# Padding the SBUF pools on both sides so that every FFN tile starts on a multiple of 1,024 bytes

## The chip, the cores and the metric

One core of a Trainium2 chip (trn2) runs the kernel. The time is device microseconds of one execution; the kernel before takes 1147.21 us (median of 3 runs, 1147.18 to 1148.46).

## What is computed

Attention with rotary embedding over 4 batches, 8 heads, 576 positions and 64 dimensions per head, then two feed-forward layers (FFN) over the 2,304 resulting tokens of width 512, with a hidden width of 2,048. All values are float32.

```python
def _attn_ref(q, k, v):            # (4, 8, 576, 64)
    ...
    scores = scale * np.matmul(q_rot, k_rot.transpose(0, 1, 3, 2))
    attn = np.exp(scores - np.max(scores, axis=-1, keepdims=True))
    attn = attn / (np.sum(attn, axis=-1, keepdims=True) + 1e-09)
    return np.matmul(attn, v)

def _moe_ref(x, w_in, w_out):      # layer 1
    h = x @ w_in
    return (h - np.tanh(h)) @ w_out

def _moe2_ref(x, w_in, w_out):     # layer 2
    h = x @ w_in
    return (h * (1.0 / (1.0 + np.exp(-h)))) @ w_out
```

## The kernel before

**Attention** goes over 16 pairs of heads, nine score tiles each. A pair's rotated queries and keys (`qs`, `kh`, `kl`, `qr`) lie in the pool `qk_even` for the pairs 0, 2, 4, ... and in `qk_odd` for the others. Once per pair a transposition `tpr` (L402) turns the reciprocals of its row sums. While attention runs, a converter (`Conv`) turns the FFN weights into a high and a low fp32r part each (L121 to L153, ACT, DVE and POOL).

**The FFN** follows from about 328 us on. Tokens are cut into five blocks `kb`: four of 512 tokens and one of 256. There are four passes `p`: passes 0 and 1 are the two halves of layer 1's hidden width, passes 2 and 3 those of layer 2. The table `SEQ` lists pass, block and `f`, one of the eight slices of 128 hidden columns of a half; each entry is one call of `tick`. A tick of a 512-token block issues two groups on TensorE:

- `gemm_h` (L685): twelve matmuls, `w_in` chunks as the weights, the block's input as the streamed operand: for each of four chunks `win` high by `xh`, `win` high by `xl`, `win` low by `xh`.
- `gemm_out` (L761) for the tick four before: three matmuls for each of `na` accumulators. In passes 0 and 1 `wout` is loaded as weights and `gh`/`gl` are streamed; in passes 2 and 3 `gh`/`gl` are loaded as weights and `wout` is streamed.

So TensorE runs twelve matmuls of L685 and twelve of L761 in turn. Before each matmul its weights (128 x 128) are loaded by an instruction of their own. Between the two groups ACT and DVE work the activation out (L696 to L730: `t`, `u`, `s`, `mk`, `gh`, `gl`). The order is written out by hand in `tick`; no table or scheduler moves it.

**Where the tiles lie.** SBUF is filled from two sides. The left side takes the pools `const`, `stage`, `wearly`, then attention's own tiles and `qk_odd`, whose place `wlate`, `ffn_out` and `ffn_x` take over after attention. The right side takes `qk_even` and `rope`, whose place the pool `ffn` takes over. A tile's address is the sum of the sizes ahead of it. In the built program `const` holds 512 + 32 + 32 bytes per partition behind a start at 16,512, so that the first tile after it, `raw`, begins at byte 17,088, which is 704 past a multiple of 1,024. All later FFN tiles of the left side (`wa`, `wm`, `win`, `wout`, `xo`, and the `xh`, `xl` of `ffn_x`) are multiples of 1,024 bytes long and begin at 704 past such a multiple as well. The right side ends at the end of SBUF; its FFN tiles (`xin`, the other `xh` and `xl`, `t`, `u`, `s`, `mk`, `gh`, `gl`) all begin at 992 past a multiple of 1,024.

An input block's `xh` and `xl` alternate between the sides (`split`, L665 to L671):

```python
        fp = pools["sb" if x % 2 == 0 else "x"]
        hi = fp.tile([128, T], F32R, tag=f"xh{c}", name=f"xh{c}", bufs=1)
        lo = fp.tile([128, T], F32R, tag=f"xl{c}", name=f"xl{c}", bufs=1)
```

`pools["sb"]` is the right side, `pools["x"]` the left; `x` counts the input blocks as they are loaded. Of the 128 ticks of 512-token blocks 72 stream their input from the right side and 56 from the left. Of those 56, 24 lie in layer 1 and 32 in layer 2. The weights `win` and `wout` are always on the left, `gh` and `gl` always on the right.

Of the kernel before, what the change touches and what calls it, by code (L numbers as in the profile page):

```python
# [8 lines left out]
F32 = mybir.dt.float32  # L9
# [20 lines left out]
def kernel(  # L30
# [39 lines left out]
    const = ctx.enter_context(tc.tile_pool(name="const", bufs=1))  # L70
# [3 lines left out]
    make_identity(nc, ident)  # L74
    sqa = const.tile([128, 1], F32, name="sqa")
    ht2 = const.tile([128, 1], F32, name="ht2")
    dram = ctx.enter_context(tc.tile_pool(name="dram", bufs=1, space=bass.MemoryType.DRAM))

    xd = [[dram.tile([128, KD, TW[kb]], F32, name=f"xd{l}{kb}") for kb in range(NBLK)] for l in range(2)]
# [820 lines left out]
```

## Time and profile before

| | |
|---|---|
| time, median of 3 runs | 1147.21 us (1147.18 to 1148.46) |
| span of the profiled execution | 1145.9 us |
| TensorE (PE) busy | 1119.5 us, 98% |
| weight loads (PEld) busy | 902.6 us, 79% |
| VectorE (DVE) busy | 785.3 us, 69% |
| ScalarE (ACT) busy | 659.2 us, 58% |
| GpSimd (POOL) busy | 268.4 us, 23% |
| mean granted TensorE clock | 0.999 |

The profile gives the profiled execution's time as its span, from the first instruction to the last; the median of the timed runs lies 1.3 us above that. A matmul's duration in the profile (about 394 ns for 512 columns) is longer than the distance from its start to the next one's start: neighbours overlap. What a matmul costs in a row of many is that distance, which the timeline shows.

### The profile page before, as it was taken

The numbers are of one execution on the slowest core, as the hardware profiler recorded it, in microseconds if no ns is written. First come the engines' busy times: TensorE is split into PE (matmuls) and PEld (weight loads), VectorE is DVE, ScalarE is ACT, GpSimd is POOL, SyncE is SP. The second block draws the span as 40 slices with busy tenths as digits, with TensorE's granted clock in tenths as the row PEclk, the third lists the DMA queues.
The fourth block names the chain that finished last, engine by engine and source line by source line (L and its number), as shares of the span: only waits on it lengthen the run. The fifth ranks groups of instructions, "written<-read, shape, count | busy, mean of one in ns | idle before, by whom it ended". The sixth has DMA issues, their size and how long they took to land.

```text
span 1145.9 us, 16928 instructions
## 1 busy us (share of the span) xinstructions
PE 1119.5 (98%) x6032; PEld 902.6 (79%) x6032; DVE 785.3 (69%) x1385; ACT 659.2 (58%) x1431; POOL 268.4 (23%) x359
## 2 busy tenths in 40 slices
PE   5999999999999999999999999999999999999998
PEld 4777777777778889888888898888888888888887
DVE  7778788787858978888899979876544533323323
ACT  4888888788866757766666657534343323222221
POOL 6566676666300101111001001111000000000000
PEclk9999999999999999999999999999999999999999
DMA  4133323232311223221333332432232203122012
GB/s 130 47 99 84 113 68 110 89 94 86 100 64 42 92 74 111 96 89 56 111 129 110 111 120 84 147 111 92 75 110 74 74 1 111 37 74 93 31 44 74
DMA packets 69588, 98.94 MB, mean 86 GB/s; under 512 B 13952, under 2 KB 50432, under 8 KB 67712
## 3 DMA queue, kind: packets, MB, share of 16 engines
q1 hardware_dynamic: 69344, 97.61, 26.3%
q8 instruction: 47, 0.77, 0.3%
q14 instruction: 37, 0.30, 0.1%
q10 hardware_dynamic: 160, 0.26, 0.1%
HBM read 74.25 MB, written 23.59 MB: 85 GB/s over the span
## 4 chain that ended last, share of the span: by engine, by line
PE 91%; DVE 4%; ACT 3%; issue 1%; DMA 0%; SPq 0%; POOL 0%; DVEq 0%; ACTq 0%
PE acc L761 35%; PE hp L685 35%; PE x L498 7%; PE tpp L466 4%; PE sc L364 3%; PE sc L365 2%; PE tpq L332 2%; PE sc L371 1%; ACT p L391 1%; DVE st L377 1%; ACT kh L346 1%; PE sc L446 1%; PE tpb L418 0%; DMA xm<-in_q_dram 0%; DVE wa L136 0%
## 5 line engine op out<-in xcount | busy, mean ns | idle before, releaser
L685 PE MATMUL hp<-xh,win 128*128 128x512 f32 (+1 forms) x1280 | 391.7, 371 | 0.0
L696 ACT ACTIVATE t<-hp 128x512 f32<-128x512 f32 (+1 forms) x160 | 89.0, 557 | 409.7 <-PE hp L685 400.0
L730 DVE TENSOR_TENSOR gl<-t,gh 128x512 fp32r<-128x512 f32 (+1 forms) x160 | 105.9, 662 | 259.5 <-ACT gh L728 259.2
L685 PEld LDWEIGHTS hp<-xh,win 128*128 128x128 f32 x1280 | 233.7, 188 | 46.8 <-issue 1.3
L685 PE MATMUL hp<-xl,win 128*128 128x512 f32 (+1 forms) x640 | 237.0, 370 | 0.0
L761 PE MATMUL acc<-gh,wout 128*128 128x512 f32 (+1 forms) x640 | 196.7, 372 | 1.2 <-ACT u L700 1.2
L761 PE MATMUL acc<-wout,gh 128*128 128x512 f32 x576 | 181.0, 395 | 0.0
L377 DVE TENSOR_REDUCE st<-sc 128x1 f32<-128x576 f32 x144 | 108.7, 755 | 60.0 <-PE sc L446 34.9
L685 PEld LDWEIGHTS hp<-xl,win 128*128 128x128 f32 x640 | 120.2, 188 | 23.2
L761 PEld LDWEIGHTS acc<-gh,wout 128*128 128x128 f32 x640 | 116.7, 188 | 24.9 <-ACT u L700 1.6
L761 PEld LDWEIGHTS acc<-wout,gh 128*128 128x128 f32 x576 | 107.1, 188 | 24.4
L761 PE MATMUL acc<-gl,wout 128*128 128x512 f32 (+1 forms) x320 | 118.9, 372 | 0.0
L153 POOL TENSOR_TENSOR win<-wa,win 128x512 fp32r<-128x512 f32 x32 | 45.4, 1419 | 292.5 <-ACT win L149 292.5
L761 PE MATMUL acc<-wout,gl 128*128 128x512 f32 x288 | 113.8, 395 | 0.0
L391 ACT ACTIVATE p<-sc,st 128x576 f32<-128x576 f32 x144 | 107.0, 743 | 9.4 <-DVE pr L434 7.2
L153 POOL TENSOR_TENSOR wout<-wa,wout 128x512 fp32r<-128x512 f32 x32 | 43.8, 1367 | 284.2 <-ACT wout L149 272.5
L432 ACT ACTIVATE pt<-tpp 128x512 f32<-128x512 f32 x144 | 86.1, 598 | 28.2 <-PE tpp L466 27.4
L728 ACT ACTIVATE gh<-t 128x512 fp32r<-128x512 f32 (+1 forms) x160 | 93.7, 586 | 1.5 <-PE acc L761 1.5
L364 PE MATMUL sc<-kh,qs 128*128 128x288 f32 x256 | 85.4, 348 | 7.1 <-ACT p L391 5.1
L466 PE MATMUL tpp<-ident,p 128*128 128x128 f32 x576 | 87.1, 274 | 0.0
L498 PE MATMUL x<-pt,vm 128*64 128x256 f32 (+1 forms) x512 | 75.8, 418 | 2.1 <-DVE xs L507 1.9
L364 PEld LDWEIGHTS sc<-kh,qs 128*128 128x128 f32 x256 | 49.2, 192 | 34.2 <-ACT p L391 17.8
(112 smaller groups left out, 1798.5 us busy)
## 6 DMA issues: line engine op xcount, KB each, us to landing
raw<-in_moe_w_in_dram SPq DMA_DIRECT2D x32, 512.0 KB, 3.6
raw<-in_moe_w_out_dram SPq DMA_DIRECT2D x32, 512.0 KB, 3.6
xin<-xd SPq DMA_DIRECT2D x14, 1024.0 KB, 4.8
pd<-xo SPq DMA_DIRECT2D x34, 256.0 KB, 2.7
xo<-pd SPq DMA_DIRECT2D x34, 256.0 KB, 4.9
xm<-in_k_dram SPq DMA_DIRECT2D x16, 256.0 KB, 2.9
xm<-in_q_dram SPq DMA_DIRECT2D x16, 256.0 KB, 3.0
vm<-in_v_dram SPq DMA_DIRECT2D x16, 256.0 KB, 2.9
```

What stands on the lines that cost most here:

```text
L153: POOL.tensor_tensor(out=w[:, 1], in0=self.val.pop(j), in1=w[:, 0].bitcast(F32), op=ALU.subtract)
L364: PE.matmul(sc[:, e, 0:HALF], lhsT=l, rhs=kh[:, c], start=True, stop=False)
L377: DVE.tensor_reduce(out=st, in_=s_t[g][:, :, 0:HALF], op=ALU.max, axis=AX.XY, negate=True)
L391: ACT.activation(out=p.rearrange("p (e s) -> p e s", e=2), in_=sc[:, :, 0:HALF], func=ACTF.Exp, bias=st, accum_out=sum_t[i][:, n:n + 1])
L432: ACT.activation(out=dst, in_=src, func=ACTF.Copy)
L466: PE.transpose(tp[:, cc * 128:(cc + 1) * 128], p[:, p0 + cc * 128:p0 + (cc + 1) * 128], ident)
L498: PE.matmul(x[o, 0:w], lhsT=l, rhs=r, start=(cc == 0), stop=(cc == NJ))
L685: PE.matmul(hp, lhsT=w[:, a, ws], rhs=bb, start=(n == 0), stop=(n == 3 * KD - 1))
L696: ACT.activation(out=t, in_=hp, func=ACTF.Tanh, scale=0.5 if l else 1.0)
L728: ACT.activation(out=gh, in_=t, func=ACTF.Copy)
L730: DVE.tensor_tensor(out=gl, in0=t, in1=gh.bitcast(F32), op=ALU.subtract)
L761: PE.matmul(acc, lhsT=a, rhs=bb, start=(fi == 0 and n == 0), stop=(fi == NH - 1 and n == 2))
```

## The change

Two tiles that nobody reads or writes are added: 80 float32 (320 bytes) per partition at the end of `const`, and a pool of its own on the right side with 248 float32 (992 bytes), opened before all others there.

```diff
     sqa = const.tile([128, 1], F32, name="sqa")
     ht2 = const.tile([128, 1], F32, name="ht2")
+    const.tile([128, 80], F32, name="pad_left")
+    right_pad = ctx.enter_context(tc.tile_pool(name="right_pad", bufs=1, side="right"))
+    right_pad.tile([128, 248], F32, name="pad_right")
     dram = ctx.enter_context(tc.tile_pool(name="dram", bufs=1, space=bass.MemoryType.DRAM))
```

Everything on the left behind `const` moves up by 320 bytes and everything on the right moves down by 992. All FFN tiles of both sides then begin on a multiple of 1,024. Tiles of one side keep their distances to each other; the distance between a tile on the right and one on the left falls by 1,312 bytes, which is just what was free between the sides. Attention's tiles move by the same amounts; those of `qk_even` come from 992, 480 and 224 past a multiple of 1,024 to 0, 512 and 256. On every engine the instructions, their order and their waits are the same as before; only addresses differ. Line numbers behind the added lines rise by 3.

## Rows read from the trace of the kernel before

**Rows 1.** Page: TensorE's busy time, and its granted clock in 40 slices
```profile
PE 1119.5 (98%) x6032; PEld 902.6 (79%) x6032; DVE 785.3 (69%) x1385; ACT 659.2 (58%) x1431; POOL 268.4 (23%) x359
...
PEclk9999999999999999999999999999999999999999
```

**Rows 2.** Groups by line and shape, TensorE: names, shapes, count | busy, mean ns | idle before
```profile
L685 PE MATMUL hp<-xh,win 128*128 128x512 f32 x1024 | 341.0, 394 | 0.0
L685 PE MATMUL hp<-xl,win 128*128 128x512 f32 x512 | 201.0, 393 | 0.0
L761 PE MATMUL acc<-wout,gh 128*128 128x512 f32 x576 | 181.0, 395 | 0.0
L761 PE MATMUL acc<-gh,wout 128*128 128x512 f32 x512 | 171.5, 396 | 1.2 <-ACT u L700 1.2
L761 PE MATMUL acc<-wout,gl 128*128 128x512 f32 x288 | 113.8, 395 | 0.0
L761 PE MATMUL acc<-gl,wout 128*128 128x512 f32 x256 | 101.1, 395 | 0.0
```

**Rows 3.** Waits of TensorE from 300 us to the end: total, times, longest
```profile
PE acc L761 <- ACT u L700: 1.2, 1, 1.2
```

**Rows 4.** Timeline of TensorE, layer 1, input on the right: start, us, instruction
```profile
717.85 0.63 PE L685 MATMUL hp<-xh,win 128*128 128x512 f32 x2
...
719.25 0.63 PE L685 MATMUL hp<-xh,win 128*128 128x512 f32 x2
...
720.65 0.63 PE L761 MATMUL acc<-gh,wout 128*128 128x512 f32 x2
...
722.05 0.63 PE L761 MATMUL acc<-gh,wout 128*128 128x512 f32 x2
```

**Rows 5.** Timeline of TensorE, layer 2, input on the left
```profile
940.79 0.61 PE L685 MATMUL hp<-xh,win 128*128 128x512 f32 x2
...
942.15 0.61 PE L685 MATMUL hp<-xh,win 128*128 128x512 f32 x2
```

**Rows 6.** Chain that ended last, in order of time: start, us, instructions
```profile
567.61 2.80 PE acc L761 x12
...
612.08 2.80 PE acc L761 x12
...
798.30 2.80 PE acc L761 x12
...
815.10 2.80 PE acc L761 x12
...
887.96 2.79 PE acc L761 x12
...
970.86 2.79 PE acc L761 x12
```

**Rows 7.** Timeline of TensorE, 256-token block: input on the right, then on the left
```profile
422.33 0.40 PE L685 MATMUL hp<-xh,win 128*128 128x256 f32 x2
...
423.04 0.40 PE L685 MATMUL hp<-xh,win 128*128 128x256 f32 x2
...
834.83 0.40 PE L685 MATMUL hp<-xh,win 128*128 128x256 f32 x2
...
835.54 0.40 PE L685 MATMUL hp<-xh,win 128*128 128x256 f32 x2
```

**Rows 8.** Windows (us, busy PE, PEld, DVE, ACT, POOL, clock, DMA); DVE's waits 560:700
```profile
570.00:590.00 20.00, 20.00 (x88) 16.21 (x87) 19.86 (x30) 12.83 (x24) 3.96 (x3) 1.00 0.41 132
...
DVE gl L730 <- ACT gh L728: 13.6, 11, 1.9
```

**Rows 9.** Timeline of TensorE: the transposition that each pair of heads has once
```profile
37.54 0.27 PE L402 MATMUL tpr<-ident,rr 128*9 128x128 f32 x1
...
56.98 0.27 PE L402 MATMUL tpr<-ident,rr 128*9 128x128 f32 x1
...
76.42 0.27 PE L402 MATMUL tpr<-ident,rr 128*9 128x128 f32 x1
```

## The prediction

> **What bounds the kernel now.** [...] Then its groups by shape: the 512-column matmuls of the FFN have no idle time ahead of them but for one wait of 1.2 us [rows 2], and from 300 us to the end that is TensorE's only wait of this size [rows 3]. From 328 us on the time is the number of matmuls times the distance between their starts. Nothing else has to be known about that stretch, and only something that alters this distance can alter the time.
>
> The change moves no instruction. So I asked the timeline whether the distance depends on where the operands lie, since the kernel itself holds a comparison: the same line, L685, with the same weights on the left, streams its input from the right side in some ticks and from the left in others.
>
> - Input on the right (it begins at 992 past a multiple of 1,024, the weights at 704): from 717.85 to 719.25 are six matmuls, 1.40 us or 233 ns each [rows 4].
> - Input on the left (704 and 704): from 940.79 to 942.15 are six matmuls, 1.36 us or 227 ns each [rows 5].
> - L761 in the same stretch as the first, streamed operand on the right, weights on the left: 720.65 to 722.05, again 1.40 us for six [rows 4].
>
> The chain of waits shows the same over whole ticks (twelve of L685 and twelve of L761). Three ticks with input on the right take 815.10 - 798.30 = 16.80 us, 5.60 each. Fifteen ticks of layer 2 with input on the left take 970.86 - 887.96 = 82.90 us, 5.527 each. Eight ticks of layer 1 with input on the left take 612.08 - 567.61 = 44.47 us, 5.559 each [rows 6]. A group of twelve of L761, whose two operands are always on different sides, takes 2.80 us. So a group of L685 takes 2.80 us with its input on the right, 2.727 us with it on the left in layer 2 and 2.759 us in layer 1. The twelve matmuls do the same arithmetic each time. What differs is the residue of the addresses: operands on one side have the same residue, operands on different sides are 288 bytes apart (992 - 704), an odd multiple of 32.
>
> **The change part by part.** After it all FFN tiles have residue 0 modulo 1,024, whichever side they are on. Every pair of streamed operand and weights then relates as those on one side do now. I therefore give every 512-column group the 2.727 us that whole groups with equal residues take in layer 2 [rows 6].
>
> - Counts. L685 has 1,024 + 512 = 1,536 matmuls of 512 columns, 128 groups of twelve; L761 has 512 + 256 in layer 1 and 576 + 288 in layer 2, 1,632 in all or 136 groups [rows 2]. Of the 128 groups 72 have their input on the right, 24 on the left in layer 1, 32 on the left in layer 2.
> - L685 with input on the right: 72 x (2.800 - 2.727) = 5.3 us less.
> - L761: 136 x 0.073 = 9.9 us less.
> - L685 with input on the left, layer 1: 24 x (2.759 - 2.727) = 0.8 us less, if the excess there is left over from the unequal group just before, as I assume (no row settles it). With input on the left in layer 2: 0.
> - The 256-column matmuls (48 groups): six take 0.71 us with input on the right and 0.71 us with it on the left [rows 7]. I take 0. The rows are rounded to 0.01 us, which is at most 1 us over all of them, either way.
> - Attention. Even pairs have their scores' operands on the right, odd pairs on the left, and both take 19.44 us from one transposition to the next [rows 9]. I take 0. The trace doesn't show a pair with both residues 0; I keep 2 us either way, 0.1 us for each of 16 pairs and a little more.
> - ACT, DVE, POOL and the DMA queues do the same work in the same order, off the path; shorter ticks reach them only through their slack (below).
> - The tail behind the last matmul, and the one wait of 1.2 us ahead of L761, stay as they are.
>
> The sum is 5.3 + 9.9 + 0.8 = 16.0 us off a span of 1145.9. I carry the 1.3 us by which the median of the runs lies above that span over unchanged: 1147.2 - 16.0 = **1131.2 us**.
>
> For the bounds of the group's new time: if all groups settle at the 1.36 us for six of rows 5, a group takes 2.72 us and the sum grows by 264 x 0.007 = 1.8 us, to 1129.4 us. If every group keeps the 2.759 us of layer 1, the gain is 208 x 0.041 less 32 x 0.032, 7.5 us, and the time 1139.7 us. I stay near the first because after the change no group of unequal residues runs ahead of any other.
>
> **The rivals.**
>
> *The residue isn't the cause* (something else about the two sides is, or the padding changes only what doesn't matter). Then every group keeps its time and the result is 1147.2 us. For it: only one difference of residues is in the trace, and it goes together with the side. Against it: streamed operands on the left are fast with weights on the left (`xh`, 2.727 us) and slow with weights on the right (`wout` in layer 2, 2.80 us), so it is the pair, not the side or the address of either alone. [...] Chance 6%.
>
> *Half of it.* The equal residues help L685 only, because L761 in layer 2 loads its weights from `gh`, four chunks in turn, a pattern that no row shows with equal residues. Then 5.3 + 0.8 us, and in layer 1 possibly 64 x 0.073 = 4.7 us more: 1136.4 to 1141.1 us. Chance 6%.
>
> *VectorE becomes the bound of layer 1.* Between 570 and 590 us it is busy 19.86 of 20 us [rows 8], and a tick that is 2.6% shorter leaves it less. If it holds TensorE back through all of layer 1, that layer's share is lost: 40 groups of L685 on the right and 64 of L761, 104 x 0.073 + 0.8 = 8.4 us, so 1139.6 us. Against it: from 560 to 700 us VectorE itself waited 13.6 us for ACT's `gh`, that is, it keeps catching up [rows 8], and TensorE waits for neither [rows 3]. Chance 4%.
>
> *Slower: equal residues lock the two reads into each other.* If the streamed operand and the weights that load at the same time now always meet in the same place of a memory row, a group could stay in the state that makes the left-side groups of layer 1 2.759 instead of 2.727 us. If that excess of 0.032 us is from the first half of a group, ran through all of it, and doubled with the right side's new addresses, a group would take 2.72 + 4 x 0.032 = 2.85 us. Now the mean group takes (208 x 2.800 + 24 x 2.759 + 32 x 2.727) / 264 = 2.787 us, so the kernel would lose 264 x 0.063 = 17 us and take 1164 us. It decides at 2.787 us for the mean group: below that the change gains. Against it: the left-side pairs already have equal residues, modulo 2,048 even, and settle at 227 ns. Chance 3%.
>
> *Better than forecast.* Residue 0 itself, not only equality, may spare more. [...] Chance 4%.
>
> **How the numbers follow.** My forecast (all groups between 2.72 and 2.759 us, attention within 2 us) has 77%, the rivals 6, 6, 4, 3 and 4%. The range reaches from 1127 us (settled everywhere, attention 2 us better) to 1140 us (the slow end of the forecast, VectorE's bound, and half of the partial case). About 0.2% of the time, 2.3 us, is what a measurement of this kernel can tell from no change. Faster by more than that: 77 + 6 + 4 + 4 = 91%. Within it: 6%. Slower: 3%.
>
> **What would show it right or wrong.** In the new timeline six matmuls of L685 and of L761 (three lines lower there) take 1.36 us each, whichever side the input is on; the chain's ticks are 5.45 us everywhere; the durations of ACT and DVE rows stay; waits of TensorE stay near 1 us. I am wrong about the cause if the ticks stay at 5.60 us, about VectorE if ticks of layer 1 show waits ahead of L761 or L685, and about the pattern if L761 of layer 2 alone stays at 1.40 us for six.

## The result and the profile after

The changed kernel takes 1130.74 us (median of 4 runs, 1130.59 to 1131.60), the kernel before 1147.20 us in the same comparison (4 runs, 1146.99 to 1148.46). The ratio is 0.9855, 95% interval 0.9841 to 0.9869: 16.5 us less, where 16.0 us had been forecast (1131.2 us).

The page of the changed kernel has a span of 1128.7 us, with TensorE as busy as before (98%) at the same granted clock (1.000, before 0.999). Its busy time fell by 17.2 us, as much as the span (compare [rows 1]):

```profile
span 1128.7 us, 16928 instructions
...
PE 1102.3 (98%) x6032; PEld 902.4 (80%) x6032; DVE 783.4 (69%) x1385; ACT 658.5 (58%) x1431; POOL 268.9 (24%) x359
...
PEclk9999999999999999999999999999999999999999
```

The timeline of TensorE in layer 1 shows the distances, in the same block and pass as [rows 4], with the input on the right (line numbers are three higher; start and duration in us):

```profile
709.27 0.62 PE L688 MATMUL hp<-xh,win 128*128 128x512 f32 x2
...
710.63 0.62 PE L688 MATMUL hp<-xh,win 128*128 128x512 f32 x2
...
711.99 0.62 PE L764 MATMUL acc<-gh,wout 128*128 128x512 f32 x2
...
713.35 0.62 PE L764 MATMUL acc<-gh,wout 128*128 128x512 f32 x2
```

Six matmuls of L688 take 710.63 - 709.27 = 1.36 us, and six of L764 take 713.35 - 711.99 = 1.36 us. Before, the six of either line took 1.40 us with operands on different sides. Sides no longer show: over the whole trace 512-column matmuls start 227.0 ns apart, those of L688 226.9 ns with input on the left and 227.0 ns with it on the right.

The chain of waits has the same groups of twelve as [rows 6]; two stretches of it, one in layer 1 with both kinds of input and one in layer 2:

```profile
512.82 2.72 PE acc L764 x12
...
621.62 2.72 PE acc L764 x12
...
851.22 2.72 PE hp L688 x12
...
932.82 2.72 PE hp L688 x12
```

Twenty ticks of layer 1 take 621.62 - 512.82 = 108.80 us, fifteen of layer 2 take 932.82 - 851.22 = 81.60 us, and both are 5.44 us a tick. Before, ticks took 5.60, 5.559 and 5.527 us [rows 6], according to side and layer.

What lies beside TensorE did not change its pace, and did not come to bind. VectorE's `gl` takes 721 ns and ScalarE's `gh` 628 ns in the groups by shape, the same as before to the nanosecond:

```profile
L733 DVE TENSOR_TENSOR gl<-t,gh 128x512 fp32r<-128x512 f32 x128 | 92.3, 721 | 204.9 <-ACT gh L731 204.8
...
L731 ACT ACTIVATE gh<-t 128x512 fp32r<-128x512 f32 x128 | 80.4, 628 | 0.0
```

The waits, of TensorE from 300 us on and of VectorE from 560 to 700 us (compare [rows 3, 8]):

```profile
PE acc L764 <- DVE xo L774: 1.3, 1, 1.3
...
DVE gl L733 <- ACT gh L731: 11.3, 10, 1.8
```

TensorE still has a single wait over 1 us in the FFN, now put down to VectorE's draining of the accumulators. VectorE still idles 11.3 us in that stretch, after 13.6 us before [rows 8]: the shorter ticks took about a sixth of its slack there.

### The profile page after: what moved, and what is told of

It is laid out like the page before. It is cut to its first block, busy times and chain, and to the rows that moved or that the text cites. A ratio compares the mean times of both kernels' runs of the same rounds, so it can differ in the third digit from the quotient of the medians.

```text
span 1128.7 us, 16928 instructions
## 1 busy us (share of the span) xinstructions
PE 1102.3 (98%) x6032; PEld 902.4 (80%) x6032; DVE 783.4 (69%) x1385; ACT 658.5 (58%) x1431; POOL 268.9 (24%) x359
## 4 chain that ended last, share of the span: by engine, by line
PE 90%; DVE 4%; ACT 3%; issue 1%; DMA 0%; POOL 0%; SPq 0%; DVEq 0%; ACTq 0%
PE acc L764 34%; PE hp L688 34%; PE x L501 7%; PE tpp L469 4%; PE sc L367 4%; PE sc L368 2%; PE tpq L335 2%; PE sc L374 2%; ACT p L394 1%; ACT kh L349 1%; DVE st L380 1%; PE sc L449 1%; PE tpb L421 1%; DVE wa L142 0%; PE tpb L425 0%
## 5 line engine op out<-in xcount | busy, mean ns | idle before, releaser
L688 PE MATMUL hp<-xh,win 128*128 128x512 f32 (+1 forms) x1280 | 387.6, 368 | 0.0
L688 PEld LDWEIGHTS hp<-xh,win 128*128 128x128 f32 x1280 | 234.3, 188 | 42.0 <-issue 1.3
L688 PE MATMUL hp<-xl,win 128*128 128x512 f32 (+1 forms) x640 | 235.5, 368 | 0.0
L764 PE MATMUL acc<-gh,wout 128*128 128x512 f32 (+1 forms) x640 | 193.7, 368 | 1.3 <-DVE xo L774 1.3
L764 PE MATMUL acc<-wout,gh 128*128 128x512 f32 x576 | 177.6, 390 | 0.0
L688 PEld LDWEIGHTS hp<-xl,win 128*128 128x128 f32 x640 | 120.6, 188 | 20.5
L764 PEld LDWEIGHTS acc<-gh,wout 128*128 128x128 f32 x640 | 117.2, 188 | 21.8 <-ACT u L703 1.7
L764 PEld LDWEIGHTS acc<-wout,gh 128*128 128x128 f32 x576 | 107.1, 188 | 21.4
L764 PE MATMUL acc<-gl,wout 128*128 128x512 f32 (+1 forms) x320 | 117.8, 368 | 0.0
L764 PE MATMUL acc<-wout,gl 128*128 128x512 f32 x288 | 112.0, 389 | 0.0
```

What stands on the lines that cost most here:

```text
L688: PE.matmul(hp, lhsT=w[:, a, ws], rhs=bb, start=(n == 0), stop=(n == 3 * KD - 1))
L764: PE.matmul(acc, lhsT=a, rhs=bb, start=(fi == 0 and n == 0), stop=(fi == NH - 1 and n == 2))
```

## The experiments

Three theories stood at first. **Difference:** only the difference between the start of the streamed operand and that of the weights counts. **Own start:** each operand has to begin on a round address by itself. **Multiple of 1,024:** the tiles have to begin on one. In all runs below the arithmetic and the order of instructions are those of the kernel before. Differences are given modulo 256, streamed right side less left side; the kernel before has (992 - 704) modulo 256 = 32, the changed kernel 0.

### Equal starts that are no multiples of 1,024

The right side alone is padded, so that it joins the left at 704:

```diff
+    right_pad = ctx.enter_context(tc.tile_pool(name="right_pad", bufs=1, side="right"))
+    right_pad.tile([128, 72], F32, name="pad_right")
```

> The right side alone is padded, by 288 bytes, so that its FFN tiles come to 704 past a multiple of 1,024, where those of the left lie already. Difference theory (only the difference of the two residues counts): all groups of twelve take 2.72 us, 1131 us. Own-start theory (each operand has to begin on a multiple of 64, and 704 is 11 x 64): 1131 us too. Multiple-of-1,024 theory (the tiles have to begin on such a multiple): no gain, 1147 us.

Measured: 1131.50 us (1130.91 to 1131.83), ratio to the kernel before 0.9862 (0.9845 to 0.9878). Neither multiples of 1,024 nor a pad on the left are needed.

Then the left side alone, so that it joins the right at 992, an odd multiple of 32:

```diff
+    const.tile([128, 72], F32, name="pad_left")
```

> The left side alone is padded, by 288 bytes, so that the FFN tiles of both sides lie at 992 past a multiple of 1,024, which is 32 past a multiple of 64. Difference theory: 2.72 us for a group, 1131 us. Own-start theory: every streamed operand and all weights are now off a multiple of 64, so no group gets faster and the 56 groups that were fast get slower: 56 x 0.06 = 3.5 us more, 1150 us. Multiple-of-1,024 theory: 1147 us or a little more.

Measured: 1132.12 us (1131.25 to 1132.81), ratio 0.9869 (0.9854 to 0.9883). Its chain has the same groups:

```profile
704.77 2.72 PE hp L686 x12
707.49 2.72 PE acc L762 x12
710.21 2.72 PE hp L686 x12
```

The own-start theory falls here: no FFN tile of this kernel begins on a multiple of 64, and of the 191 groups of twelve that its chain lists 166 take 2.72 us and 21 take 2.75 us.

### Which differences are as good as none

A difference of 256, by a pad of 32 bytes on the right alone:

```diff
+    right_pad.tile([128, 8], F32, name="pad_right")
```

> The right side alone is padded, by 32 bytes: right at 960, left at 704, a difference of 256; both are multiples of 64. Modulo-64 forms of the difference and the own-start theory: 2.72 us for a group, 1131 us. Equality modulo 1,024, or multiples of 1,024, as the condition: 1147 us, as the residues are neither equal nor 0.

Measured: 1131.14 us (1130.71 to 1131.54), ratio 0.9860 (0.9846 to 0.9875). With both pads of the change replaced by 32 bytes, the whole gain is there.

The changed kernel with its right pad 32 bytes shorter, so that the difference is 32 again:

```diff
-    right_pad.tile([128, 248], F32, name="pad_right")
+    right_pad.tile([128, 240], F32, name="pad_right")
```

> The changed kernel with the right pad 32 bytes shorter: left at 0, right at 32. Modulo-64 theories, difference or own start: groups with operands on different sides take 2.80 us again, all of the gain is lost, 1147 us. If it were closeness of the residues in steps coarser than 32 bytes that counts: 1131 us.

Measured: 1146.97 us (1145.90 to 1148.43), ratio 0.9999 (0.9990 to 1.0009): the kernel before, with its left tiles on multiples of 1,024. A period of 64 bytes fitted these four runs and was the reading behind the expectations of most of the others. Two more runs tested it. A difference of 64:

```diff
+    right_pad.tile([128, 56], F32, name="pad_right")
```

> The right side alone is padded, by 224 bytes: right at 768, left at 704, a difference of 64. If the pattern repeats every 64 bytes: 2.72 us for a group, 1131 us. If it repeats every 128 or 256 bytes (the equal cases so far differed by 0 or 256): slower than that, up to 1147 us.

Measured: 1142.74 us (1141.45 to 1143.78), ratio 0.9965 (0.9950 to 0.9980). The period of 64 falls. The timeline says more than the time. It has L763 in a tick of layer 1, where `gh` is streamed, and in one of layer 2, where `wout` is:

```profile
716.09 0.62 PE L763 MATMUL acc<-gh,wout 128*128 128x512 f32 x2
...
717.47 0.62 PE L763 MATMUL acc<-gh,wout 128*128 128x512 f32 x2
...
905.51 0.63 PE L763 MATMUL acc<-wout,gh 128*128 128x512 f32 x2
...
906.91 0.63 PE L763 MATMUL acc<-wout,gh 128*128 128x512 f32 x2
```

Six matmuls of L763 take 1.38 us in layer 1 and 1.40 us in layer 2. In layer 1 the streamed `gh` lies 64 ahead of the weights' start, in layer 2 the streamed `wout` lies 64 behind it (192 modulo 256). Over the whole trace the 512-column matmuls of L763 start 229.5 ns apart in layer 1 and 233.4 ns in layer 2. Those of L687 with input on the right, 64 ahead, start 229.0 ns apart in layer 1 and 231.3 ns in layer 2, 230.0 ns in the mean. So the size of the difference counts, and at 64 also which operand lies ahead. At 32 and 128 that counts for little: in the kernel before L761 takes 233.4 ns with the streamed operand 32 ahead (layer 1) and 233.1 ns with it 32 behind (layer 2), and L763 takes 233.0 and 232.7 ns at a difference of 128 (the next run).

The groups with input on the left have a difference of 0 here, and still take 230.6 ns in layer 1 and 229.2 ns in layer 2: a good difference alone doesn't give 227 ns. The section on one line at a time shows where that comes from.

A difference of 128:

```diff
+    right_pad.tile([128, 40], F32, name="pad_right")
```

> The right side alone is padded, by 160 bytes: right at 832, left at 704, a difference of 128. A difference of 64 has given 1142.7 us, one of 256 has given 1131 us. If the pattern repeats every 128 bytes: 2.72 us for a group, 1131 us. If it repeats only every 256 bytes: groups with operands on different sides take more than 2.76 us, 1138 to 1147 us.

Measured: 1146.79 us (1145.92 to 1147.55), ratio 0.9994 (0.9984 to 1.0004). Nothing is gained. The timeline has groups of 713.45 to 716.25 and 716.25 to 719.05 us, 2.80 us each:

```profile
713.45 0.40 PE L763 MATMUL acc<-gh,wout 128*128 128x512 f32 x1
...
716.25 0.40 PE L687 MATMUL hp<-xh,win 128*128 128x512 f32 x1
...
719.05 0.40 PE L763 MATMUL acc<-gh,wout 128*128 128x512 f32 x1
```

Of the differences tried, 0 and 256 give the whole gain, 64 a part, and 32 and 128 none. The chunks of one weight tile lie 512 bytes apart, and all of them are fast against one streamed tile: in the changed kernel the distances at each of the twelve places of a group of L688 are 226.2 to 228.9 ns in the mean. A period of 256 bytes fits all of this; other differences were not measured by themselves. Multiples of 1,024 are one way to meet it.

A difference of 16 was tried by using `xh`, `xl` of the right side, `gh` and `gl` from the fifth element of tiles 64 bytes longer, behind a pad of 32 bytes:

```diff
+    right_pad.tile([128, 8], F32, name="pad_right")
...
+        if x % 2 == 0:
+            hi, lo = (fp.tile([128, T + 16], F32R, tag=f"{n}{c}", name=f"{n}{c}", bufs=1)[:, 4:4 + T] for n in ("xh", "xl"))
...
-        gh, gl = tmp(m, "gh", 3, F32R), tmp(m, "gl", 3, F32R)
+        w = TW[SEQ[m][1]]
+        gh, gl = (pools["sb"].tile([128, T + 16], F32R, tag=n, name=n, bufs=3)[:, 4:4 + w] for n in ("gh", "gl"))
```

> xh, xl of the right side, gh and gl begin 16 bytes past a multiple of 64 (each tile 64 bytes longer, used from its fifth element on), the left stays at 704. If only the 32-byte half counts in which an operand begins: 2.72 us for a group, 1131 us. If the cost grows with the difference from 0 to 32: about half of it, 1139 us. If any difference costs the same: 1147 us. [...]

Measured: 1145.00 us (1144.23 to 1145.93), ratio 0.9981 (0.9971 to 0.9991). This run doesn't answer its question. It was made when the period was thought to be 64; the longer tiles put neighbouring tiles 64 bytes out of step, so that the right-side streams of L685, say, have differences of 16, 80, 144 and 208 in turn. What a difference of 16 costs by itself stays open.

### One line at a time

In the kernel before, 32 bytes are added inside the right-hand FFN pool just ahead of `gh` and `gl`. The right side's `xh` and `xl` come to 960, 256 from the left's 704, and only `gh` and `gl` stay at 992:

```diff
+        if m == 0:
+            pools["sb"].tile([128, 8], F32, name="pad_g")
         gh, gl = tmp(m, "gh", 3, F32R), tmp(m, "gl", 3, F32R)
```

> The kernel before with 32 bytes of padding inside the right-hand FFN pool, just ahead of gh and gl: xh and xl of the right side come to 960 (a multiple of 64, as the left's 704), gh and gl stay at 992. Only the groups of L685 gain. Difference theory with the terms of the prediction: 5.3 + 0.8 = 6.1 us less, 1141.1 us, groups of L761 still 2.80 us. If the gain of the two lines comes only when the whole stream is equal, nothing is gained: 1147 us.

Measured: 1144.01 us (1143.22 to 1144.56), ratio 0.9970 (0.9959 to 0.9982): 3.4 us, not 6.1. The timeline of a tick of layer 1 shows what is missing:

```profile
716.03 0.40 PE L685 MATMUL hp<-xh,win 128*128 128x512 f32 x1
...
716.49 0.63 PE L685 MATMUL hp<-xh,win 128*128 128x512 f32 x2
...
717.19 0.63 PE L685 MATMUL hp<-xh,win 128*128 128x512 f32 x2
...
717.88 0.62 PE L685 MATMUL hp<-xh,win 128*128 128x512 f32 x2
...
718.56 0.39 PE L685 MATMUL hp<-xh,win 128*128 128x512 f32 x1
718.78 0.40 PE L763 MATMUL acc<-gh,wout 128*128 128x512 f32 x1
```

Three matmuls take 0.70 us at the group's start, then 0.69, then 0.68. A group with a good difference starts at the old pace when the group ahead of it had a bad one, and settles in the course of some seven matmuls. The group takes 718.78 - 716.03 = 2.75 us instead of 2.72. The seven are no constant: in layer 2 of this run only the first distance is long (231 ns, then 227), and in the run with a difference of 64 the left-side groups of layer 1 settle after ten.

The complement puts `gh` and `gl` at 960 and the right side's `xh` and `xl` at 928, with the pad above and one of 32 bytes at the start of the right side:

```diff
+    right_pad.tile([128, 8], F32, name="pad_right")
...
+        if m == 0:
+            pools["sb"].tile([128, 8], F32, name="pad_g")
```

> The complement: gh and gl at 960, xh and xl of the right side at 928 (32 past a multiple of 64). Only the 136 groups of L761 gain. Difference theory: 136 x 0.073 = 9.9 us less, 1137.3 us, and with the run that leaves gh and gl off it adds up to the whole gain. If the whole stream has to be equal: 1147 us.

Measured: 1138.43 us (1138.09 to 1138.62), ratio 0.9923 (0.9908 to 0.9937), 8.9 us less than the kernel before. The right side's input lies 32 behind the weights here (224 modulo 256), and its 512-column matmuls start 233.5 ns apart, as at 32 ahead. The two halves give 3.4 + 8.9 = 12.3 us, where both together give 16 us. The traces show where the missing 4 us are: the distances of L685 fall by 3.8 us with `gh` and `gl` off, and those of L761 by 8.5 us in the complement, where the changed kernel has 6.6 and 10.1 us. The rest is lost to the switches between bad and good groups, of which the changed kernel has none.

### A version that goes further

With a bad difference the 256-column matmuls are faster, not slower: over the whole trace those streaming from the right side start 117.6 ns apart before, and 119.7 ns after the change. So the changed kernel was given back its 32 bytes for the 256-token block alone:

```diff
+        o = 8 if w < T else 0
+        hi, lo = (fp.tile([128, T], F32R, tag=f"{n}{c}", name=f"{n}{c}", bufs=1)[:, o:o + w] for n in ("xh", "xl"))
...
-        gh, gl = tmp(m, "gh", 3, F32R), tmp(m, "gl", 3, F32R)
+        w = TW[SEQ[m][1]]
+        o = 8 if w < T else 0
+        gh, gl = (pools["sb"].tile([128, T], F32R, tag=n, name=n, bufs=3)[:, o:o + w] for n in ("gh", "gl"))
```

> The changed kernel, but the 256-token block uses its xh, xl, gh and gl from the ninth element on, 32 bytes past a multiple of 64. In the changed kernel's trace 256-column matmuls start 119.6 ns apart, in that of before 117.6 ns where the residues differ. Difference theory: 576 x 2 ns = 1.2 us less than the changed kernel, 1129.6 us. If the 256-column rate hangs on something else: 1130.7 us as the changed kernel, or slower by up to 1 us if the switches between blocks cost.

Measured: 1130.03 us (1129.44 to 1130.43), ratio to the kernel before 0.9849 (0.9835 to 0.9864). In its trace 256-column matmuls start 116.8 ns apart on either side, and six of them take 419.95 - 419.25 = 0.70 us (0.72 us in the changed kernel):

```profile
419.25 0.39 PE L688 MATMUL hp<-xh,win 128*128 128x256 f32 x2
...
419.95 0.39 PE L688 MATMUL hp<-xh,win 128*128 128x256 f32 x2
```

To set it against the changed kernel both were run once more on one chip:

> The changed kernel once more, beside the run with the 256-token block 32 bytes off, on one chip: 1130.7 us by both theories.

> The changed kernel with the 256-token block's operands 32 bytes past a multiple of 64, once more beside the changed kernel. Its first trace has 576 matmuls of 256 columns at 116.8 instead of 119.6 ns, 1.6 us in all. If that reaches the end: 1129.1 us, 1.6 us under the changed kernel. If the switches between blocks give part of it back: 0.5 to 1 us under it.

Measured: 1131.34 us (1131.20 to 1131.40) for the changed kernel and 1130.49 us (1129.93 to 1130.62) with the block off by 32. All four runs of the second lie under all four of the first, by 0.85 us in the medians; that is 0.08% and less than the 0.2% I would trust from one comparison. In the trace the 576 matmuls save 1.6 us. The same block's 96 matmuls of L766 in layer 2 give back 0.4 us (233.2 ns apart, 229.0 in the changed kernel): they stream 512 columns of `wout` against chunks of `gh` that now lie 32 bytes off. Leaving `gh` and `gl` of layer 2 where they were was not tried.

## Why the prediction was right, step by step

- *Nothing but the distance between matmuls counts from 328 us on.* Right. The sums of the distances over the two traces: 512-column matmuls of L761 380.2 us before and 370.1 after, 10.1 us less (forecast 9.9); those of L685 353.3 and 346.7, 6.6 us less (forecast 5.3 + 0.8 = 6.1). Distances over 300 ns, of which there are nine in either trace, are waits or have other matmuls between, and are left out.
- *Every group takes 2.727 us.* Slightly too much: 2.72 us, the lower bound that the text gave. In layer 1 the excess of the left-side groups was, as assumed there, left over from the unequal group just ahead. The run with `gh` and `gl` off shows this, since it gives that excess to the right-side groups too (2.755 us, and 2.754 us on the left). In layer 2 part of the excess over 2.72 us came from the group's last matmul instead (below).
- *The 256-column matmuls: 0, at most 1 us either way.* They cost: 68.1 us before, 68.9 after, 0.8 us more, within that bound. This miss and the 0.2 and 0.5 us that the two lines gained above their terms partly cancel: 10.1 + 6.6 - 0.8 = 15.9 us. That it comes so close to the 16.0 us of the sum is in part luck. Six take 0.72 us in the changed kernel's timeline (0.71 in [rows 7]):

```profile
419.15 0.40 PE L688 MATMUL hp<-xh,win 128*128 128x256 f32 x2
...
419.87 0.40 PE L688 MATMUL hp<-xh,win 128*128 128x256 f32 x2
```

- *Attention: 0.* Right. From one `tpr` to the next are 19.42 us now (55.59 to 75.01), 19.44 before [rows 9]. In the profiled execution of the changed kernel the first FFN matmul starts 1.4 us earlier, nearly all of it gained ahead of the first `tpr`; in the second run of the same kernel 0.5 us of that was there. Over all traces here that start lies between 326.3 and 327.8 us, at 327.6 us in a run with the whole gain and at 326.3 us in one with next to none, so I don't count it to the change. From the first FFN matmul to the last one's start the time fell from 813.0 to 797.3 us, 15.7 us less; with the earlier start that makes up the 17.2 us of the span but for rounding. The medians, 16.5 us apart, take in other executions.

```profile
55.59 0.27 PE L405 MATMUL tpr<-ident,rr 128*9 128x128 f32 x1
...
75.01 0.27 PE L405 MATMUL tpr<-ident,rr 128*9 128x128 f32 x1
```

- *VectorE's bound* did not come: its slack shrank from 13.6 to 11.3 us over 140 us and TensorE's one wait went from 1.2 to 1.3 us. *Half of it* did not come either: L761 of layer 2, whose weights are chunks of `gh`, went from 233.1 to 227.0 ns a matmul, that of layer 1 from 233.4 to 227.0 ns. *Locking into each other* did not come: groups settle at 2.72 us, not at 2.85. *Better than forecast* did not come: residue 0 itself spares nothing more, 227 ns a matmul and 1130.74 us, where equal residues of 704 gave 1131.50 us and of 992 1132.12 us.
- *The residue isn't the cause* did not come. The runs in which addresses alone moved speak against it: 32 bytes ahead of the right side of the kernel before gave 1131.14 us instead of 1147 us, and 32 bytes fewer there in the changed kernel 1146.97 us instead of 1131 us. Weight loads run beside matmuls here: in the traces before and after, 3,739 of the 3,744 loads of the two lines begin and end within the matmul ahead of their own, 188 ns each in the mean. That this load, of the next matmul's weights, takes part is what the run with `gh` and `gl` off speaks for: in layer 2 the last matmul of a group of L685 has a good difference to its own weights, and a bad one to those of `gh` that load beside it. Its distance to the next start is 235 ns in the median, against 227 ns for the eleventh (0.24 and 0.23 us in the lines below). In layer 1, where the next weights are `wout`, the last one has 227 ns as well.

```profile
795.90 0.39 PE L685 MATMUL hp<-xl,win 128*128 128x512 f32 x1
796.13 0.40 PE L685 MATMUL hp<-xh,win 128*128 128x512 f32 x1
796.37 0.62 PE L763 MATMUL acc<-wout,gh 128*128 128x512 f32 x2
```

That it is this load does not come out at every difference. In the same place, with input on the left, the run with a difference of 128 has 232 ns, but that with a difference of 64, where the streamed input lies 64 behind the next weights, has 226 ns, although whole groups at 64 behind take 233.4 ns. So the pace is shown to hang on the addresses; whether it is the load that slows the matmul, and how, stays open.

- One reading in the prediction was too narrow: it took the harm to lie in "an odd multiple of 32". The forecast rested only on equal residues and so did not suffer, but a difference of 128 costs as much as one of 32. It also speaks of equal residues modulo 1,024, "modulo 2,048 even", on one side. That holds for the starts of tiles at most: the weights that a matmul reads are chunks 512 bytes apart, so fast operands differed by multiples of 512 already.

## What to carry to other kernels

Where TensorE is bound by a row of float32r matmuls with a weight load before each, compare the distance between starts for the same line with its operands in different places before anything else; a kernel that keeps buffers of one kind on both sides of SBUF, as this one does, holds the comparison in its own trace. Here a pad of 32 bytes on one side, which makes the starts of streamed tiles and weight tiles differ by a multiple of 256 bytes, is worth 1.4% of the whole kernel. Try several paddings, since neither a round address (1131.50 us with all tiles at 704, 1132.12 us at 992) nor a small difference (1147 us at 32, 1131.14 us at 256) is what counts here, and the shorter matmuls want the opposite (256 columns: 116.8 ns at 32, 119.6 ns at 0).

## What the runs showed that was not expected

- The pace of 512-column matmuls depends on the difference of two addresses, not on either address: 227 ns apart at a difference of 0 modulo 256, 233 ns at 32 or 128.
- At 64 the sign of the difference counts: the streamed operand 64 ahead gives 229.0 to 231.3 ns by line and layer, 64 behind gives 233.4 ns. At 32 and 128 either sign gives about 233 ns. At 64 the sign goes with the side that the weights are on in these runs, so the two are not told apart.
- The pace has a memory: after a group with a bad difference a good one needs between one and ten matmuls to settle, seven in layer 1 after a difference of 32 (three take 0.70 us at the group's start and 0.68 us at its end).
- 256-column matmuls go the other way: 119.6 ns at a difference of 0, 116.8 ns when their operands lie 32 bytes off.
- In the settled state 512 columns take 226.7 ns (2.72 us for twelve) and 256 columns 120 ns (0.72 us for six). A straight line through the two, an estimate from these two lengths alone, has 106.7 ns for 256 columns, 0.417 ns a column, and 13.3 ns on top per matmul. What these go to isn't shown by these runs.
